# Sparse attention and a two-layer MLP on one core: score pieces of a head pair joined, an order of pieces rewritten, a copy placed later

## The chip, the cores and the metric

One Trainium2 chip, one of its cores. The metric is the device time of one execution in microseconds (us). Twelve runs of the kernel before gave a median of 329.03 us (328.61 to 331.29).

## What is computed

Attention over 8 batches, 8 heads, 576 positions and head size 64. Heads 0 to 3 are *local* (a query sees the 32 positions up to itself), heads 4 to 7 are *strided* (a query sees earlier positions with the same remainder modulo 32). The result, with heads side by side, is a matrix of 4608 rows and 512 columns, which goes through two matrix products with a leaky activation between them.

```python
scores = scale * np.matmul(q, k.transpose(0, 1, 3, 2))
mask_local = (rel >= 0) & (rel < stride)
mask_strided = (rel >= 0) & (pos[None, :] % stride == pos[:, None] % stride)
attn = softmax(where(mask, scores, -1e9))
x = matmul(attn, v).transpose(0, 2, 1, 3).reshape(B * S, H * D)
h = x @ w_in
g = np.maximum(h, 0.0) + alpha * np.minimum(h, 0.0)
out = g @ w_out
```

## The kernel before

**Units.** Heads are taken in pairs; pair g = 4*batch + hp, where hp 0 and 1 are local, 2 and 3 strided. The two heads of a pair lie on partitions 0 to 63 and 64 to 127 of qT and kT. Only blocks that the mask leaves are computed: 6 query blocks of 96 (local) or 8 of 72 (strided) per head. The MLP works in 9 chunks of 512 rows; chunk n needs the attention result up to its last row. `xT`, a ring of four batches, carries the attention result, transposed, from one to the other; its second index is hp.

**A pair's pieces.**
- T, `transpose_piece` and `tails` (L221 to L273): q and k of two pairs are transposed on TensorE into banks of the PSUM pool "ps" (three banks), then copied by DVE and ScalarE. From batch 2 on (`DX`) strided q and k are transposed by DMA instead (`load_d`, `transpose_d`, on SP's queue).
- S, `score_piece` (L275 to L329), two per pair: matmuls with 64 rows, one head on the upper and one on the lower half of the array (L295). Then an exp on ScalarE: one instruction of 576 columns (L319) from the double bank "sp" (pool "pb", one buffer) or, while `wide` is on and for every second piece, two of 288 (L316) from two banks of the pool "ph". In batches 0 and 1 the mask is added by two further matmuls (L311); later GpSimd (POOL) multiplies the exps by a 0/1 mask (L329).
- P, `pv_piece` (L331 to L357), two or three per pair: exps times V with a column of ones (L345) into a "ps" bank; DVE takes the reciprocal of the sum (L352) and multiplies (L354) into x16.
- X: `x_piece` (L359) transposes x16 on TensorE and copies it to xT, by ScalarE for strided (L366) and by DVE for local pairs (L370). For hp 0, 1 and 2 of batches 2 and up a transposing DMA does it: `x_dma` (L372) on SP's queue, straight into xT for local pairs, and for hp 2 into `xs`, which ScalarE copies to xT (`x_copy`, L380, L383).

**MLP pieces.** `lin1_piece` (L534): four matmuls of 512 columns (L544), one for each hp, into one of three banks of "ph"; ScalarE computes relu(-h) (L554), and DVE combines (L557). The DVE half is kept in `late` and issued by the next `attn_step`. `lin2_piece` (L563): four matmuls (L585); every fourth is followed by ScalarE's copy (L590) and the store (L591).

**Order.** The program order of each engine is the order of the Python calls (`keep`). Batch 0 runs alone at the start, with warm matmuls (L607) between its pieces. Batch 1 is woven into chunk 0's lin2 pieces. `alone(u0, u1, ahead)` (L406) writes out the order of these two batches. From batch 2 on the loop of L449 feeds the pieces of each step g in the order S(g,0), P(g-1,0), T q, X(g-2), S(g,1), P(g-1,1), T k, P(g-1,2), and hangs loads, casts, `x_dma`, `transpose_d` and `x_copy` on them. `attn_step` (L524) issues one piece; the loop of L708 issues a batch's pieces evenly over a chunk's 32 MLP pieces, at half density in the lin1 half. During chunk n it issues batch n + 1.

Of the kernel before, what the change touches and what calls it, by code (L numbers as in the profile page):

```python
# [9 lines left out]
F32 = mybir.dt.float32  # L10
F16 = mybir.dt.float16
ALU = mybir.AluOpType
AF = mybir.ActivationFunctionType
# [18 lines left out]
def kernel(  # L32
# [140 lines left out]
    def cast_copy(eng, o, i):  # L173
        if eng == "act":
            keep(nc.scalar.copy(o, i))  # L175
        elif eng == "dve":
            keep(nc.vector.tensor_copy(o, i))  # L177
        else:
            keep(nc.gpsimd.tensor_copy(o, i))  # L179
# [9 lines left out]
    def over_v(b, eng):  # L189

        v16 = vls[b % 2]
        cast_copy(eng, v16[0:32, 1:24, :], v16[96:128, 0:23, :])
# [82 lines left out]
    def score_piece(P, i):  # L275
# [52 lines left out]
            m = (mstr if P.strided else mother).unsqueeze(1).to_broadcast([r, 2 * n // w, w])  # L328
        keep(nc.gpsimd.tensor_tensor(ev, ev, m, op=ALU.mult))  # L329

    def pv_piece(P, a):  # L331
        if P.x16 is None:
            if P.xd and P.strided:
                P.x16 = x16s
            else:
                P.x16 = xpool.tile([128, 1024], F16, tag="x16", name="x16")
        v16 = cast16[(P.b, P.strided, "v")]
        grp = P.pgroups[a]
        r = 72 if P.strided else 128
        pv = pspool.tile([128, 512], F32, tag="ps", name="pv")  # L340
        nb = 2 * len(grp)
        for x in range(nb):
            t, hh = grp[x // 2], x % 2
            et, c = P.et[(t, hh)]
            keep(nc.tensor.matmul(  # L345
                pv[:, 65 * x : 65 * x + 65], et[0:r, c : c + 128],
                v16[0:r, 2 * P.pr + hh, t, :] if P.strided else v16[:, 6 * (2 * P.pr + hh) + t, :],
                start=(x == 0), stop=(x == nb - 1), skip_group_check=True))
        w = P.w
        rc = rpool.tile([128, 8], F32, tag="rc", name="rc")  # L350
        pvv = pv[0:w, 0 : 65 * nb].rearrange("r (c e) -> r c e", e=65)
        keep(nc.vector.reciprocal(rc[0:w, 0:nb], pvv[:, :, 64]))  # L352
        c0 = 128 * grp[0]
        keep(nc.vector.tensor_tensor(  # L354
            P.x16[0:w, c0 : c0 + 64 * nb].rearrange("r (c e) -> r c e", e=64),
            pvv[:, :, 0:64],
            rc[0:w, 0:nb].unsqueeze(2).to_broadcast([w, nb, 64]), op=ALU.mult))  # L357

    def x_piece(P):  # L359
        xp = pspool.tile([128, 1024], F16, tag="ps", name="xp")  # L360
        for t in range(P.n):
            keep(nc.tensor.transpose(  # L362
                xp[:, P.w * t : P.w * t + P.w], P.x16[0 : P.w, 128 * t : 128 * t + 128], ident[0 : P.w, 0 : P.w]))
        base = (P.b % 4) * S
        if P.strided:
            keep(nc.scalar.copy(  # L366
                xT[:, P.hp, base : base + S].rearrange("r (p t) -> r p t", t=8),
                xp[:, 0:576].rearrange("r (t p) -> r p t", t=8)))
        else:
            keep(nc.vector.tensor_copy(xT[:, P.hp, base : base + S], xp[:, 0:576]))  # L370

    def x_dma(P):  # L372
        base = (P.b % 4) * S
# [7 lines left out]
    def x_copy(P):  # L381
        base = (P.b % 4) * S
        keep(nc.scalar.copy(  # L383
            xT[:, P.hp, base : base + S].rearrange("r (p t) -> r p t", t=8),
            P.xs[:, :, 0:72].rearrange("r t p -> r p t")))
# [5 lines left out]
    def feed(fn, g):  # L391
        pieces.append((g, fn))

    def T(u, nm):
        return lambda: transpose_piece(u, nm)

    def Sc(g, i):
        return lambda: score_piece(pairs[g], i)

    def Pv(g, i):  # L400
        return lambda: pv_piece(pairs[g], i)

    def X(g):
        return lambda: x_piece(pairs[g])

    def alone(u0, u1, ahead):  # L406

        A, L = (2 * u0, 2 * u0 + 1), (2 * u1, 2 * u1 + 1)
        feed(T(u0, "q"), -1)
        feed(T(u0, "k"), -1)  # L410
        for g in A:
            for i in range(2):
                feed(Sc(g, i), -1)
        if ahead:
            feed(T(u1, "q"), -1)
            feed(T(u1, "k"), -1)
            for i in range(2):
                feed(Sc(L[0], i), -1)
        for g in A:
            for i in range(3):  # L420
                feed(Pv(g, i), -1)
        if not ahead:
            feed(T(u1, "q"), -1)
            feed(X(A[0]), -1)
            feed(T(u1, "k"), -1)
            feed(X(A[1]), -1)
            for i in range(2):
                feed(Sc(L[0], i), -1)
        for i in range(2):
            feed(Sc(L[1], i), -1)  # L430
        if ahead:
            for g in A:
                feed(X(g), -1)
        for g in L:
            for i in range(2):
                if g == L[0] and i == 0:
                    feed(lambda: (over_v(u0 // 2, "dve"), pv_piece(pairs[L[0]], 0)), -1)
                else:
                    feed(Pv(g, i), -1)
        for g in L:  # L440
            feed(X(g), -1)

    alone(1, 0, True)
    end0 = len(pieces)
    alone(3, 2, True)
    end1 = len(pieces)


    for g in range(7, npair + 2):  # L449
        c = g // 4  # L450
        a, p, t = g, g - 1, g + 1
        okA = 8 <= a < npair
        okP = 8 <= p < npair
        okT = 8 <= t < npair and (t % 4 == 0 or t < 4 * DX and t % 2 == 0)
        nP = len(pairs[p].pgroups) if okP else 0
        seq = []
        if okA:
            seq.append(("S", Sc(a, 0)))
        if okP:
            seq.append(("P", Pv(p, 0)))  # L460
        if okT:
            seq.append(("T", T(t // 2, "q")))
        if 8 <= g - 2 < npair and not pairs[g - 2].xd:
            seq.append(("X", X(g - 2)))
        if okA:
            seq.append(("S2", Sc(a, 1)))
        if okP:
            seq.append(("P", Pv(p, 1)))
        if okT:
            seq.append(("Tk", T(t // 2, "k")))  # L470
        if nP == 3:
            seq.append(("P", Pv(p, 2)))
        if not seq:
            seq.append(("N", lambda: None))

        todo = [(c, pr) for pr in range(2)] if g % 4 == 0 and 8 <= g < npair else []

        if g % 4 == 1 and 9 <= g and c + 1 < B:
            todo = [(c + 1, nm) for nm in "qk"]
        lastP = max([i for i, z in enumerate(seq) if z[0] == "P"], default=len(seq) - 1)  # L480
        copyP = next((i for i, z in enumerate(seq) if z[0] == "S2"), 0)
        nslots = [i for i, z in enumerate(seq) if z[0][0] != "S"] or list(range(len(seq)))
        for i, (kind, fn) in enumerate(seq):
            extra = []
            if todo and i in nslots:
                left = len([z for z in nslots if z >= i])
                cnt = -(-len(todo) // max(1, left))
                extra = [todo.pop(0) for _ in range(min(cnt, len(todo)))]

            def run(fn=fn, extra=extra, g=g, c=c, kind=kind, lastp=(i == lastP), copyp=(i == copyP)):  # L490
                fn()
                for b, pr in extra:
                    if pr in ("q", "k"):
                        cast_l(b, pr)
                        if b + 1 < B:
                            load_qk(b + 1, False, pr)
                        continue
                    cast_v(b, pr, "pool")
                    if pr == 1 and b + 1 < B:
                        load_v(b + 1, True)  # L500
                if kind == "Tk" and g % 4 == 3 and c + 3 < B:
                    load_tail(c + 3, False)
                if lastp:
                    if 4 * DX <= g - 1 < npair and pairs[g - 1].xd:
                        x_dma(pairs[g - 1])
                    if g % 4 == 0 and DX <= c < B:
                        transpose_d()
                    if g % 4 == 2 and DX <= c and c + 1 < B:
                        load_d(c + 1)
                    if g % 4 == 2 and c + 2 < B:  # L510
                        load_v(c + 2, False)
                if copyp and 4 * DX <= g - 2 < npair and pairs[g - 2].xd and pairs[g - 2].strided:
                    x_copy(pairs[g - 2])
            feed(run, g - 2 if kind == "X" else -1)

    pos = {"i": 0}
# [7 lines left out]
    def attn_step(end):  # L524
        if pos["i"] < end:
            pieces[pos["i"]][1]()
            pos["i"] += 1
        while late:
            late.pop(0)()


    gTs = {}
# [222 lines left out]
```

The softmax here doesn't subtract the row's maximum and nothing guards it: scores larger than these inputs give would overflow.

## Time and profile before

| | us |
|---|---|
| median of 12 runs | 329.03 |
| the profiled execution, its own time | 329.14 |
| its span, first to last instruction | 327.20 |
| batch 0 alone, until the first lin1 matmul | 0 to 26.7 |
| chunk 0: lin1, then lin2 with batch 1 | 26.7 to 40.8, 40.8 to 65.2 |
| chunk 1 with batch 2 | 65.2 to 101 |
| one later chunk with a batch, from 136.5 to 169.9 | 33.4 |
| chunks 7 and 8, without attention | 268.1 to the end |

Busy times by engine over the span are 317.4 us for TensorE's matmuls (PE), 182.8 for DVE, 172.5 for ScalarE (ACT) and 141.2 for POOL; the granted TensorE clock is 1.00 throughout. In the lines that follow, a timeline row gives the start, the duration, engine, source line and tiles of one instruction or of a run of like ones (xN), and in brackets how long the engine was idle before and for whom. A group row gives busy time and mean. A row of waits gives engine and tile that waited, whom it waited for, the total in us, how often, and the longest. PEld is TensorE's weight load.

### The profile page before, as it was taken

What the parts mean: (1) busy time and instruction counts of PE and PEld (TensorE: products, weight loads), DVE (VectorE), ACT (ScalarE), POOL (GpSimd) and SP (SyncE); (2) the same over time, 40 slices, a digit from 0 to 9 for tenths busy, and PEclk for the clock granted to TensorE, in tenths of its full rate; (3) what the DMA queues carried; (4) which work ended last, traced back from release to release, by engine and by line L of the source; (5) the groups of instructions that cost most, each with busy time, mean ns of one, the idle gap of its engine ahead of it and who ended that gap; (6) DMA issues with size and microseconds to landing.
All of it is one profiled execution on the core that took longest, in us unless ns stands there. A gap on an engine that the chain in (4) does not pass through costs nothing.

```text
span 327.2 us, 6269 instructions
## 1 busy us (share of the span) xinstructions
PE 317.4 (97%) x2493; PEld 161.7 (49%) x2493; DVE 182.8 (56%) x358; ACT 172.5 (53%) x295; POOL 141.2 (43%) x152
## 2 busy tenths in 40 slices
PE   7899999999998999999999999999999999999995
PEld 2454445554553445444568754445444454444444
DVE  5477835577543882388328833783377338505801
ACT  2744663368446754575467645764567346415610
POOL 8832396307996365736573638342513300000000
PEclk9999999999999999999999999999999999999999
DMA  7999999795498879695968496635440220021011
GB/s 223 193 206 207 248 202 181 110 266 155 94 162 138 220 78 155 98 232 68 165 107 223 53 135 123 114 38 106 119 75 3 52 89 29 1 88 40 2 64 64
DMA packets 77596, 40.32 MB, mean 123 GB/s; under 512 B 58480, under 2 KB 69248, under 8 KB 77568
## 3 DMA queue, kind: packets, MB, share of 16 engines
q0 software_dynamic: 41728, 17.38, 53.9%
q1 hardware_dynamic: 35840, 22.55, 28.9%
q8 instruction: 19, 0.31, 0.5%
q14 instruction: 9, 0.07, 0.1%
HBM read 38.01 MB, written 9.44 MB: 145 GB/s over the span
## 4 chain that ended last, share of the span: by engine, by line
PE 92%; DVE 2%; ACT 2%; DMA 2%; issue 1%; SPq 0%; DVEq 0%; ACTq 0%
PE hps L544 38%; PE ops L585 37%; PE sp L295 4%; PE pv L345 4%; PE tp L235 2%; DMA ql<-in_q_dram 2%; PE wps L607 1%; PE ops L577 1%; PE xp L362 1%; DVE x L354 1%; PE sph L311 1%; PE sp L311 1%; ACT kT L175 1%; DVE qT L177 1%; PE sph L295 1%
## 5 line engine op out<-in xcount | busy, mean ns | idle before, releaser
L585 PE MATMUL ops<-wout,gT 128*128 128x512 f16 x560 | 137.7, 379 | 0.0
L557 DVE SCALAR_TENSOR_TENSOR gT<-neg,oma,hps 128x512 f16<-128x512 f32 x144 | 106.0, 745 | 55.1 <-ACT neg L554 47.6
L544 PE MATMUL hps<-xT,win 128*128 128x512 f16 (+1 forms) x640 | 133.5, 358 | 1.8 <-ACT xT L366 1.2
L554 ACT ACTIVATE neg<-hps 128x512 f32<-128x512 f32 x144 | 86.0, 597 | 41.0 <-PE hps L544 39.5
L329 POOL TENSOR_TENSOR et<-et,consts 128x576 f16<-128x576 f16 (+1 forms) x48 | 61.1, 1275 | 92.3 <-ACT et L319 92.2
L544 PEld LDWEIGHTS <-win 128*128 128x128 f16 x640 | 59.6, 98 | 58.2 <-issue 3.2
L585 PEld LDWEIGHTS <-gT 128*128 128x128 f16 x560 | 48.4, 97 | 45.5
L319 ACT ACTIVATE et<-sp 72x576 f16<-72x576 f32 (+1 forms) x56 | 36.1, 646 | 45.0 <-PE sp L295 36.7
L352 DVE RECIPROCAL rc<-pv 72x6 f32<-72x6 f32 (+2 forms) x80 | 14.8, 185 | 51.2 <-PE pv L345 51.2
L590 ACT COPY osb<-ops 128x512 f32<-128x512 f32 x35 | 20.5, 586 | 31.6 <-PE ops L585 30.9
L354 DVE TENSOR_TENSOR x<-pv,rc 96x384 f16<-96x384 f32 (+2 forms) x62 | 33.0, 532 | 2.1
L345 PEld LDWEIGHTS <-et 72*128 72x128 f16 (+1 forms) x448 | 23.2, 98 | 16.2 <-DVE x L354 1.1
L295 PEld LDWEIGHTS <-kT 64*128 64x128 f16 x448 | 10.8, 95 | 25.8 <-issue 20.7
L295 PE MATMUL sp<-qT,kT 64*128 64x72 f16 (+1 forms) x392 | 17.0, 201 | 1.9 <-ACT kT L175 1.9
L607 PE MATMUL wps<-wrm 128*128 128x512 f16 x44 | 16.4, 448 | 1.2 <-DVE wrm L619 1.2
L345 PE MATMUL pv<-vs,et 72*128 72x65 f16 x256 | 15.3, 194 | 0.1
L167 POOL DMA_DIRECT2D vl<-in_v_dram x8 | 11.2, 1398 | 9.1 <-PE pv L345 8.0
L179 POOL COPY vs<-stv 72x1024 f16<-72x1024 f16 x14 | 14.4, 1034 | 0.0
L177 DVE COPY qT<-tp 128x1024 f16<-128x1024 f16 (+1 forms) x10 | 10.1, 1011 | 7.7 <-PE tp L235 7.7
L383 ACT COPY xT<-xs 128x576 f16<-128x576 f16 x6 | 7.8, 1300 | 8.2 <-DMA xs<-x16s 8.2
L345 PE MATMUL pv<-vl,et 128*128 128x65 f16 x192 | 10.8, 194 | 0.0
L175 ACT COPY kT<-tp 128x1024 f16<-128x1024 f16 (+1 forms) x10 | 8.4, 843 | 3.9 <-PE tp L235 3.9
(72 smaller groups left out, 162.5 us busy)
## 6 DMA issues: line engine op xcount, KB each, us to landing
out_dram<-osb SPq DMA_DIRECT2D x35, 256.0 KB, 2.3
ql<-in_q_dram SPq DMA_DIRECT2D x6, 512.0 KB, 4.7
kl<-in_k_dram SPq DMA_DIRECT2D x6, 512.0 KB, 5.2
stv<-in_v_dram POOLq DMA_DIRECT2D x8, 288.0 KB, 6.3
vl<-in_v_dram POOLq DMA_DIRECT2D x6, 384.0 KB, 10.1
win<-in_moe_w_in_dram POOLq DMA_DIRECT2D x4, 512.0 KB, 10.3
wout<-in_moe_w_out_dram POOLq DMA_DIRECT2D x4, 512.0 KB, 17.5
qsd<-in_q_dram POOLq DMA_DIRECT2D x6, 288.0 KB, 5.9
```

What stands on the lines that cost most here:

```text
L295: keep(nc.tensor.matmul(sps[y][:, w * x : w * x + w], P.kT[hf, k0 : k0 + 128], P.qT[hf, q0 : q0 + w], start=(x == 0), stop=(x == len(grp) ...
L319: keep(nc.scalar.activation(ev.rearrange("r (y c) -> r y c", y=2), sp[0:r, :, 0:n], AF.Exp, scale=SCALE))
L329: keep(nc.gpsimd.tensor_tensor(ev, ev, m, op=ALU.mult))
L345: keep(nc.tensor.matmul(pv[:, 65 * x : 65 * x + 65], et[0:r, c : c + 128], v16[0:r, 2 * P.pr + hh, t, :] if P.strided else v16[:, 6 * (2 * ...
L352: keep(nc.vector.reciprocal(rc[0:w, 0:nb], pvv[:, :, 64]))
L354: keep(nc.vector.tensor_tensor(P.x16[0:w, c0 : c0 + 64 * nb].rearrange("r (c e) -> r c e", e=64), pvv[:, :, 0:64], rc[0:w, 0:nb].unsqueeze ...
L544: keep(nc.tensor.matmul(hps[:, dst : dst + w], win16[:, kk, 128 * m : 128 * m + 128], xT[:, kk, src : src + w], start=(kk == 0 and x == 0) ...
L554: keep(nc.scalar.activation(neg, hps, AF.Relu, scale=-1.0))
L557: keep(nc.vector.scalar_tensor_tensor(gTs[n][:, m, :], neg, oma[:, m : m + 1], hps, op0=ALU.mult, op1=ALU.add))
L585: keep(nc.tensor.matmul(ops, gTs[n][:, kf, 128 * mt : 128 * mt + 128], wout16[:, kf, :], start=(kf == 0), stop=(kf == 15)))
L590: keep(nc.scalar.copy(osb, ops))
L607: keep(nc.tensor.matmul(wps, wrm[:, 0:128], wrm, start=True, stop=True))
```

## The change

Five edits:

1. From batch 2 on a new `score_both` computes both score pieces of a pair one after the other, where S(g,0) stood; S(g,1) is gone from the step. The first half uses the double bank "sp" and one exp of 576 columns, as before. The second half uses two banks of the pool "ps" and two exps of 288, which are put in `defer` and issued one at each following `attn_step` (the first at the end of the same step). `pv_piece` issues any that are outstanding for its own pair first. A pair's attention has one piece less, so the pieces of a batch are spread over the chunk at a lower density.
2. `alone` is rewritten: the PVs of the strided pairs stand between the transposes and scores of the local ones, and the local PVs between the x transposes.
3. In batches 0 and 1 the copy of pair hp 0 to xT goes to ScalarE instead of DVE.
4. `x_copy` is issued after the first piece of step g for pair g - 3; before, it was after S(g,1) for pair g - 2.
5. The local V of a batch is loaded at step 4c + 1 for batch c + 1, where it was step 4c + 2 for batch c + 2; it uses POOL's queue as before.

```diff
+    defer, defer_et = [], {}
+
+    def score_both(P):
+        w, r = P.w, 72 if P.strided else 128
+        for i in range(2):
+            et = ets[ectr["i"] % NE]
+            ectr["i"] += 1
+            if i:
+                sps = [pspool.tile([128, 512], F32, tag="ps", name="sph") for _ in range(2)]
+            else:
+                sp = pbpool.tile([128, 2, 512], F32, tag="sp", name="sp")
+                sps = [sp[:, y] for y in range(2)]
...
+            if i == 0:
+                keep(nc.scalar.activation(
+                    ev.rearrange("r (y c) -> r y c", y=2), sp[0:r, :, 0:n], AF.Exp, scale=SCALE))
+                keep(nc.gpsimd.tensor_tensor(mv, mv, m, op=ALU.mult))
+                continue
+
+            def ex(y):
+                keep(nc.scalar.activation(
+                    ev[:, n * y : n * y + n], sps[y][0:r, 0:n], AF.Exp, scale=SCALE))
+                if y:
+                    keep(nc.gpsimd.tensor_tensor(mv, mv, m, op=ALU.mult))
+
+            defer_et["et"] = et
+            defer.extend([lambda: ex(0), lambda: ex(1)])
+
     def pv_piece(P, a):
+        while defer and any(P.et[z][0] is defer_et["et"] for z in P.et):
+            defer.pop(0)()
...
-            keep(nc.vector.tensor_copy(xT[:, P.hp, base : base + S], xp[:, 0:576]))
+            cast_copy("act" if P.b < NEARLY and P.hp == 0 else "dve",
+                      xT[:, P.hp, base : base + S], xp[:, 0:576])
...
+        fns = [T(u0, "q"), T(u0, "k")] + [Sc(g, i) for g in A for i in range(2)]
+        fns += [Pv(A[0], 0), T(u1, "q"), Pv(A[0], 1), T(u1, "k"), Pv(A[0], 2), Sc(L[0], 0), Sc(L[0], 1)]
+        fns += [lambda: (over_v(u0 // 2, "dve"), pv_piece(pairs[A[1]], 0)), Sc(L[1], 0), Pv(A[1], 1)]
+        fns += [Sc(L[1], 1), Pv(A[1], 2), Pv(L[0], 0), X(A[0]), Pv(L[0], 1), X(A[1])]
+        fns += [Pv(L[1], 0), Pv(L[1], 1), X(L[0]), X(L[1])]
...
-            seq.append(("S", Sc(a, 0)))
+            seq.append(("S", lambda a=a: score_both(pairs[a])))
...
-        if okA:
-            seq.append(("S2", Sc(a, 1)))
...
-                    if g % 4 == 2 and c + 2 < B:
-                        load_v(c + 2, False)
-                if copyp and 4 * DX <= g - 2 < npair and pairs[g - 2].xd and pairs[g - 2].strided:
-                    x_copy(pairs[g - 2])
+                    if g % 4 == 1 and DX < c and c + 1 < B:
+                        load_v(c + 1, False)
+                if first and 4 * DX <= g - 3 < npair and pairs[g - 3].xd and pairs[g - 3].strided:
+                    x_copy(pairs[g - 3])
...
         while late:
             late.pop(0)()
+        if defer:
+            defer.pop(0)()
```

The order of `alone` before (A are the two strided pairs, L the two local ones): T q and T k of A, four scores of A, T q and T k of L, two scores of the first L, six PVs of A, two scores of the second L, X of both A, four PVs of L (with `over_v`, a copy of V's overlap, before the first), X of both L.

More of the change, by code (lines that the diff above doesn't have):

```diff
@@ L329, in score_piece @@
         keep(nc.gpsimd.tensor_tensor(ev, ev, m, op=ALU.mult))
+    defer, defer_et = [], {}
[9 more added lines that the diff above has]
+                sps = [sp[:, y] for y in range(2)]
+            grp = P.sgroups[i]
+            n = w * len(grp)
+            for x, t in enumerate(grp):
+                if P.dx:
+                    q0 = k0 = 80 * (4 * (2 * P.pr + t % 2) + t // 2)
+                else:
+                    q0, k0 = w * t, 32 + 72 * t if P.strided else 96 * t
+                for y in range(2):
+                    hf = slice(64 * y, 64 * y + 64)
+                    keep(nc.tensor.matmul(
+                        sps[y][:, w * x : w * x + w], P.kT[hf, k0 : k0 + 128],
+                        P.qT[hf, q0 : q0 + w], start=(x == 0), stop=(x == len(grp) - 1),
+                        skip_group_check=True))
+                    P.et[(2 * (t // 2) + y, t % 2) if P.strided else (t, y)] = (et, n * y + w * x)
+            ev = et[0:r, 0 : 2 * n]
+            if not P.strided and i == 0:
+                mv = ev.rearrange("r (y c) -> r y c", y=2)
+                m = mfirst.unsqueeze(1).to_broadcast([r, 2, n])
+            else:
+                mv = ev.rearrange("r (c f) -> r c f", f=w)
+                m = (mstr if P.strided else mother).unsqueeze(1).to_broadcast([r, 2 * n // w, w])
+            if i == 0:
[10 more added lines that the diff above has]
+            defer.extend([lambda: ex(0), lambda: ex(1)])
@@ L404, in X, with alone @@
         return lambda: x_piece(pairs[g])
-    def alone(u0, u1, ahead):
+    def alone(u0, u1):
         A, L = (2 * u0, 2 * u0 + 1), (2 * u1, 2 * u1 + 1)
[L409 to L443, printed above, removed]
+        fns = [T(u0, "q"), T(u0, "k")] + [Sc(g, i) for g in A for i in range(2)]
[3 more added lines that the diff above has]
+        fns += [Pv(L[1], 0), Pv(L[1], 1), X(L[0]), X(L[1])]
+        for fn in fns:
+            feed(fn, -1)
+    alone(1, 0)
     end0 = len(pieces)
-    alone(3, 2, True)
+    alone(3, 2)
     end1 = len(pieces)
@@ L480 @@
         lastP = max([i for i, z in enumerate(seq) if z[0] == "P"], default=len(seq) - 1)
-        copyP = next((i for i, z in enumerate(seq) if z[0] == "S2"), 0)
         nslots = [i for i, z in enumerate(seq) if z[0][0] != "S"] or list(range(len(seq)))
@@ L488, with run @@
                 extra = [todo.pop(0) for _ in range(min(cnt, len(todo)))]
-            def run(fn=fn, extra=extra, g=g, c=c, kind=kind, lastp=(i == lastP), copyp=(i == copyP)):
+            def run(fn=fn, extra=extra, g=g, c=c, kind=kind, lastp=(i == lastP), first=(i == 0)):
                 fn()
```

## The prediction, on record before the result

> **What bounds the kernel now.** I read the page first (busy shares and the chain that ended last), then the waits, then TensorE's own order of time.
>
> ```profile
> PE 317.4 (97%) x2493; PEld 161.7 (49%) x2493; DVE 182.8 (56%) x358; ACT 172.5 (53%) x295; POOL 141.2 (43%) x152
> PE 92%; DVE 2%; ACT 2%; DMA 2%; issue 1%; SPq 0%; DVEq 0%; ACTq 0%
> ```
>
> TensorE (PE) is busy 97% of 327.2 us and makes 92% of the chain; no other engine passes 56%. Only two things shorten the kernel: time that PE spends on its own account, and the few places where it waits. The waits show the first kind:
>
> ```profile
> PEld L295 <- issue: 20.7, 54, 0.4
> ```
>
> 54 times the weight load of a score matmul stood still with no semaphore to blame. In TensorE's order of time around two score visits and a PV piece:
>
> ```profile
> 138.31 0.81 PE L544 MATMUL hps<-xT,win 128*128 128x512 f16 x3
> 139.05 0.30 PE L295 MATMUL sp<-qT,kT 64*128 64x96 f16 x6
> 139.29 0.61 PE L544 MATMUL hps<-xT,win 128*128 128x512 f16 x2
> ...
> 141.03 0.35 PE L345 MATMUL pv<-vl,et 128*128 128x65 f16 x6
> 141.21 1.89 PE L544 MATMUL hps<-xT,win 128*128 128x512 f16 x8
> 143.03 0.30 PE L295 MATMUL sp<-qT,kT 64*128 64x72 f16 x8
> 143.27 0.61 PE L544 MATMUL hps<-xT,win 128*128 128x512 f16 x2
> ```
>
> A 512-column matmul starts every 0.216 us. Three from 138.31 free the array at 138.96; the scores start at 139.05: 0.095 us lost. They are three couples of 96 columns, each couple side by side on the two row halves; the last couple starts at 139.15 and streams 0.04, yet L544 starts at 139.29: again 0.095 lost. The second visit loses as much, the PV piece nothing (141.03 + 8 x 0.216 and its 0.18 lead to 142.94, and the scores start at 143.03). So a visit to the row-tiled mode costs 0.19 us beside its matmuls.
>
> The second kind is one place of some size:
>
> ```profile
> 101.12 0.59 PE L544 MATMUL hps<-xT,win 128*128 128x512 f16 x2
> 102.10 0.38 PE L544 MATMUL hps<-xT,win 128*128 128x512 f16 x1 [0.39 <-ACT xT L383]
> 103.67 1.02 PE L544 MATMUL hps<-xT,win 128*128 128x512 f16 x4 [1.19 <-ACT xT L366]
> ```
>
> Chunk 2's third matmul is due at 101.55 and starts at 102.10, its fourth is due at 102.32 and starts at 103.67: 0.55 + 1.35 = 1.9 us lost. ScalarE is behind it:
>
> ```profile
> 100.75 1.30 ACT L383 COPY xT<-xs 128x576 f16<-128x576 f16 x1 [4.23 <-DMA xs<-x16s]
> 101.96 0.58 ACT L590 COPY osb<-ops 128x512 f32<-128x512 f32 x1
> 102.44 0.65 ACT L319 ACTIVATE et<-sp 128x576 f16<-128x576 f32 x1
> 102.98 0.64 ACT L366 COPY xT<-xp 128x576 f16<-128x576 f16 x1
> ```
>
> x_copy (L383) stood 4.23 us for its transposing DMA with an output copy, an exp and the copy of pair 11 queued behind it. The DMA was issued at 93.98 and took 6.7 us here, against a median of 3.2.
>
> **The Trainium skill.** "TensorEngine Tiling (Array Packing)", Key Properties: changing the tiling mode, not just the tile, drains TensorE. The trace agrees and prices it: 0.095 us on each side. "ScalarE: Activation LUTs", What ACT_TABLE_LOAD costs: an ACTIVATE with immediate scale and bias takes 186 ns + 0.833 ns per element, and back-to-back ones overlap by 93 ns. The trace has 650 ns for 576 columns and 400 to 410 for 288, with starts 0.1 us earlier than the ends: agrees. "TensorE: Matmul & The Clock Gate", its table: ScalarE's queue is a strict FIFO; agrees with the four rows above. "DMA: Bandwidth & Descriptors", Issuing engines are not separate DMA queues: all transfers share 16 engines; the 6.7 us landing beside a V load issued at 89.19 fits that, without proving it.
>
> **The change part by part.**
>
> *One score visit for a head pair, 24 pairs of batches 2 to 7.* 48 visits become 24; none of the 48 touches another in PE's order. 24 x 0.19 = 4.5 us, all on PE, no cover: a clear gain. Matmuls stay the same in number and size. Bounds: 4.5, and 0 if the drain were paid between the two halves. I take 4.5. It adds ScalarE work: 24 exps of 576 columns become 48 of 288, 24 x (2 x 0.405 - 0.645) = 4.0 us on an engine that is 53% busy. Queued behind them is the relu L554, which frees one of three hps banks through L557. After a visit: relu of the piece before, exp 0.54 apart, half exp 0.31, then the next relu, due 1.13 us after the visit's end (0.864 of matmul + 0.27) and free at about 0.93. The second half exp is held back one piece and fits before the following relu. So no wait, with 0.2 us to spare. If ScalarE's starts were a full duration apart, about 0.25 us would be lost in each visit of the lin1 halves, 11 visits: 2.8 us (first rival).
>
> *PSUM.* The second half now takes two of the three ps banks, which PV, transposes and x results share. Along the order after the change each bank's reader has at least one 0.864 us lin piece plus other PE work before reuse; a PV's readers take 0.19 + 0.55 us, the half exps are done about 1.5 us after the visit. I cost it at nothing; the cover is the lin piece. The exception is chunk 1, where the k transposes of batch 3 now stand one lin2 piece (not two) ahead of the first visit that reads them: about 1.25 us on PE, against 1.75 from the start of such transposes to the scores at 72.58/74.33. Loss 0.5 us.
>
> *x_copy one pair later.* In chunk 1 it moves from the third piece after its DMA's issue to the fifth; five lin2 pieces (4.3), a visit (0.5), PVs (0.5) and the exp ahead make about 6.3 us, and the V load of 89.19 is no longer issued there. The 1.9 us go; I leave 0.1 for the half exps that it now delays, as the bank they free is needed by pair 11's x transposes. If the landing stays at 6.7 from the issue, up to 1.2 comes back. Also in chunk 1 the first visit comes one lin1 piece later, so two waits of scores (0.24 at 74.34, 0.09 at 77.70) vanish. With the 0.5 from above: 1.9 + 0.3 - 0.5 - 0.1 = 1.6 us gain (bounds 0.4 to 2.2).
> In the last batch nothing follows pair 31, so x_copy of pair 30 is now issued *after* pair 31's copy:
>
> ```profile
> 267.01 0.42 PE L362 MATMUL xp<-consts,x 72*128 72x72 f16 x8
> 267.27 1.03 PE L585 MATMUL ops<-wout,gT 128*128 128x512 f16 x4
> 268.13 0.81 PE L544 MATMUL hps<-xT,win 128*128 128x512 f16 x3
> ```
>
> L366 starts at 267.47; x_copy 0.52 later, 1.30 long, done at 269.3. Chunk 7's third matmul (kk = 2) wants it at 268.13 + 0.43 = 268.56. New wait: 0.8 us (0.5 to 1.3).
>
> *Batch 0.* Before, PE waits for kT 0.97 us at 16.15 with nothing else to do, and later DVE cannot keep up with ten PVs nearly in a row (0.69 us each on DVE, 0.40 on PE with the warm matmul): 0.25, 0.14, 0.28, 0.21, 0.55 and 0.27 us. Sum 2.7. After, PVs fill the first hole and DVE works from 14 us. Walking the new order with these durations, I lose about 0.5 where the tail transposes wait for the q bank (DVE copy, then ScalarE copy, now behind a PV's DVE work), 0.3 at the first chunk's second matmul and 0.3 at the last x transposes; lin1 starts near 25.3 instead of 26.68. One DVE copy (0.45) going to ScalarE is in that. I take 1.2 (0 to 1.9): the pv needs V's cast at 13.4, only 0.2 before it is due, and V's local load must land by 18 instead of 22.
>
> *Batch 1.* Two waits, 0.44 at 45.10 and 0.54 at 51.59. The first stays, the second shrinks: 0.4 gain (-0.3 to 0.8).
>
> *V load moved* to three steps later: on POOL's queue and the DMA engines; V is needed a whole batch (33 us) later and lands within 11.3. Nothing.
>
> **Sum.** 4.5 + 1.6 + 1.2 + 0.4 - 0.8 = 6.9 us. The profiled execution took 329.14 (span 327.20 and 1.94 around it), so 320.3 span and 322.2; the median of the runs, 329.03, is 0.1 less: 322.1.
>
> **Rivals.** (1) ScalarE backlog, 2.8 us as above: 324.9. Against it: starts overlap in the trace, and L544 waited only 1.8 us in all. (2) The drain belongs to each change of PSUM banks or half, so that a merged visit keeps it: 322.1 + 4.5 = 326.6. Against: couples within a visit follow each other at 0.03 to 0.05 us although they alternate banks. (3) The ps pool turns the gain over: with two of three banks held until the deferred half exps have run, each visit or the PV behind it waits for one exp of 0.405 us: 24 x 0.405 = 9.7, 331.8. It decides from 6.9/24 = 0.29 us per visit. Against: in the steady chunks the new order never reuses a bank less than 1.2 us of PE work after it was filled, and ScalarE is half idle. (4) Start and chunk 1 give nothing (inputs or the xs transfer still late): 322.1 + 1.2 + 1.6 = 324.9.
>
> **How the numbers follow.** Main case 0.66; (1) 0.11; (2) 0.08; (3) 0.05; (4) 0.08; no change 0.02. Low end: all upper bounds, 0.7 + 0.6 + 0.4 + 0.3 more, gives 320.1; the range up to 325.4 takes in (1) and (4) with half a microsecond and leaves out (2), (3) and no change, 0.15. A measurement of this kernel can tell about 0.2% (0.7 us) from no change: faster 0.93, within 0.02, slower 0.05.
>
> **What would show it.** Right: 24 fewer score visits and the issue wait of L295 down by about 24 x 0.4; a steady chunk at 32.6 instead of 33.4 us; no PE wait for L383's successor at chunk 2, but one of 0.8 at chunk 7; lin1's first matmul near 25.3. Wrong: PE waits on ACT exps or on pv's readers inside visits (3), hps waits in lin1 stretches (1), or chunks still at 33.4 (2).

## The result, and the profile after

| | before | after |
|---|---|---|
| median, us | 329.07 (32 runs) | 323.58 (8 runs, 323.33 to 323.74) |
| ratio, with 95% interval | | 0.983 [0.981, 0.984] |
| profiled execution: its time, its span | 329.14, 327.20 | 323.41, 321.63 |
| first lin1 matmul starts at | 26.68 | 25.17 |
| chunk 0 / 1 / 2 | 38.55 / 35.89 / 35.25 | 38.39 / 35.69 / 32.90 |
| chunk 3 / 4 / 5 / 6 | 33.35 / 33.52 / 33.35 / 31.54 | 32.91 / 33.04 / 32.90 / 30.78 |
| chunk 7 | 27.63 | 28.42 |

5.5 us were gained where 6.9 were forecast. (A chunk lasts from its first lin1 matmul to that of the next; the stretch from chunk 8 on is 31.43 us in both.)

The page after, in the rows that the forecast began with (busy us, share of the span, instructions; then the engines' shares of the chain that ended last):

```profile
PE 313.3 (97%) x2493; PEld 162.4 (50%) x2493; DVE 183.5 (57%) x356; ACT 172.8 (54%) x321; POOL 140.6 (44%) x152
PE 87%; issue 5%; POOL 2%; DVE 2%; DMA 2%; ACT 1%; SPq 0%; POOLq 0%; ACTq 0%; DVEq 0%
```

TensorE still bounds the kernel: the same 2493 matmuls, 97% busy. ScalarE has 26 more instructions and 0.3 us more busy time. Its exps, added one by one, take 46.8 us instead of 42.6, close to the 4.0 more of the forecast; the busy time hardly grows because ScalarE's instructions overlap more (their durations sum to 185.1 us after and 179.6 before). TensorE's weight loads, in the waits after:

```profile
PEld L353 <- issue: 8.9, 22, 0.4
PEld L569 <- issue: 3.9, 10, 0.9
PEld L295 <- issue: 3.0, 10, 0.4
```

Before, 54 loads of score weights stood still for "issue", 20.7 us in all; now it is 22 + 10, 11.9 us: 8.8 less, where the forecast's sign was about 24 x 0.4 = 9.6. The second row belongs to lin1 and is the part that the forecast missed. A visit and the stretch ahead of it, in TensorE's order of time (chunk 3):

```profile
138.18 1.90 PE L569 MATMUL hps<-xT,win 128*128 128x512 f16 x8
139.91 0.35 PE L396 MATMUL pv<-vl,et 128*128 128x65 f16 x6
140.10 2.95 PE L569 MATMUL hps<-xT,win 128*128 128x512 f16 x12
142.89 0.35 PE L396 MATMUL pv<-vl,et 128*128 128x65 f16 x6
143.07 2.75 PE L569 MATMUL hps<-xT,win 128*128 128x512 f16 x12
145.76 0.30 PE L353 MATMUL sp<-qT,kT 64*128 64x72 f16 x8
145.90 0.30 PE L353 MATMUL sph<-qT,kT 64*128 64x72 f16 x8
```

The two halves of a visit follow each other without a hole (145.76 and 145.90). From the 512-column matmul ahead of a visit (its start plus 0.216 us) to the start of the next one after the visit, the median was 0.329 us (local) or 0.332 (strided) for each of two visits before, and is 0.457 or 0.462 for the joined one: 0.20 us less per pair, 24 x 0.20 = 4.8 us. But the twelve lin1 matmuls from 140.10 show 2.95 us where those from 143.07 show 2.75: the first twelve lost 0.20. That is the new wait, two per chunk in chunks 2 to 6; in chunk 6 the kernel before had two as well, so eight of the ten are new.

The stall at the start of chunk 2 is gone:

```profile
99.25 2.75 PE L569 MATMUL hps<-xT,win 128*128 128x512 f16 x12
```

Before, the third and fourth matmuls of that chunk came 0.55 and 1.35 us late. What is left as waits of TensorE's matmuls in the middle and at the end (engine and tile, whom it waited for, us, times, longest):

```profile
PE hps L569 <- ACT xT L435: 0.6, 1, 0.6
PE pv L396 <- POOL et L375: 0.4, 1, 0.4
...
PE xp L413 <- ACT et L372: 0.2, 1, 0.2
```

The first is the end of the last batch, as forecast:

```profile
261.12 0.64 ACT L417 COPY xT<-xp 128x576 f16<-128x576 f16 x1 [2.39 <-PE xp L413]
...
261.65 1.31 ACT L435 COPY xT<-xs 128x576 f16<-128x576 f16 x1
261.78 0.59 PE L569 MATMUL hps<-xT,win 128*128 128x512 f16 x2
...
263.01 2.32 PE L569 MATMUL hps<-xT,win 128*128 128x512 f16 x10 [0.63 <-ACT xT L435]
```

The third matmul of chunk 7 (kk = 2) was due at 262.21 and starts at 263.01, when x_copy of pair 30, behind the copy of pair 31, is done: 0.80 us.

**Where the new 0.20 us comes from.** One such place in chunk 2, all engines that touch lin1:

```profile
101.84 0.35 PE L396 MATMUL pv<-vl,et 128*128 128x65 f16 x6
...
102.02 2.95 PE L569 MATMUL hps<-xT,win 128*128 128x512 f16 x12
102.04 0.60 ACT L579 ACTIVATE neg<-hps 128x512 f32<-128x512 f32 x1 [0.27 <-PE hps L569]
102.47 0.18 DVE L403 RECIPROCAL rc<-pv 96x6 f32<-96x6 f32 x1
102.69 0.55 DVE L405 TENSOR_TENSOR x<-pv,rc 96x384 f16<-96x384 f32 x1
103.08 0.60 ACT L579 ACTIVATE neg<-hps 128x512 f32<-128x512 f32 x1 [0.45 <-PE hps L569]
103.16 2.16 DVE L582 SCALAR_TENSOR_TENSOR gT<-neg,oma,hps 128x512 f16<-128x512 f32 x3
...
103.95 0.53 PEld L569 LDWEIGHTS <-win 128*128 128x128 f16 x3 [0.32 <-issue]
```

The lin1 piece ahead of the PV has its relu (L579) from 102.04 to 102.64. Its second half, DVE's combine (L582), is kept in `late` and issued by the next `attn_step` *after* that step's piece, here a PV; so it stands in DVE's queue behind the PV's reciprocal and multiplication and starts at 103.16, not at 102.64. It ends at about 103.9. Only then is its hps bank free, of which there are three; the third lin1 piece after the PV (102.02 + 2 x 0.864 = 103.75) wants the same bank and starts at 103.95. ScalarE is not late: each of its relus waited for TensorE (the brackets). The Trainium skill's "TensorE: Matmul & The Clock Gate", Part 1, lists ScalarE's and VectorE's queues as strict FIFOs; the order on DVE above agrees.

So three theories went to the chip: (A) the order on DVE, and not ScalarE, costs the 0.2 us; (B) the joined visits' gain is the drain between modes, and not a lower cost of something else; (C) what removed the 1.9 us at chunk 2, the later copy (edit 4) or, as a rival, the V load that no longer runs beside the xs transfer (edit 5). The kernel before, measured beside each group of experiments, had medians of 329.06 to 329.22 us; the intervals are those of the ratio to it. When a number is called a chunk's, it is of the profiled execution.

### The profile page after: what moved, and what is told of

Same layout as the page of the kernel before. It is cut to its first block, busy times and chain, and to the rows that moved or that the text cites. A ratio compares the mean times of both kernels' runs of the same rounds, so it can differ in the third digit from the quotient of the medians.

```text
span 321.6 us, 6320 instructions
## 1 busy us (share of the span) xinstructions
PE 313.3 (97%) x2493; PEld 162.4 (50%) x2493; DVE 183.5 (57%) x356; ACT 172.8 (54%) x321; POOL 140.6 (44%) x152
## 4 chain that ended last, share of the span: by engine, by line
PE 87%; issue 5%; POOL 2%; DVE 2%; DMA 2%; ACT 1%; SPq 0%; POOLq 0%; ACTq 0%; DVEq 0%
PE ops L610 36%; PE hps L569 35%; PE pv L396 4%; PE tp L235 2%; PE wps L632 2%; PE sp L353 2%; DMA ql<-in_q_dram 2%; PE ops L602 1%; PE xp L413 1%; PE sp L311 1%; PE sph L311 1%; PE sph L353 1%; DVE x L405 1%; PE sp L295 1%; POOL vs L179 1%
## 5 line engine op out<-in xcount | busy, mean ns | idle before, releaser
L582 DVE SCALAR_TENSOR_TENSOR gT<-neg,oma,hps 128x512 f16<-128x512 f32 x144 | 106.3, 745 | 52.6 <-ACT neg L579 44.5
L610 PE MATMUL ops<-wout,gT 128*128 128x512 f16 x560 | 135.3, 379 | 0.0
L569 PE MATMUL hps<-xT,win 128*128 128x512 f16 (+1 forms) x640 | 132.7, 358 | 1.1 <-ACT xT L435 0.6
L579 ACT ACTIVATE neg<-hps 128x512 f32<-128x512 f32 x144 | 86.0, 597 | 38.8 <-PE hps L569 38.8
L569 PEld LDWEIGHTS <-win 128*128 128x128 f16 x640 | 60.2, 98 | 60.2 <-issue 3.9
L610 PEld LDWEIGHTS <-gT 128*128 128x128 f16 x560 | 49.2, 97 | 47.2
L396 PEld LDWEIGHTS <-et 72*128 72x128 f16 (+1 forms) x448 | 24.1, 98 | 16.6 <-POOL et L375 0.9
L366 ACT ACTIVATE et<-sp 128x576 f16<-128x576 f32 (+1 forms) x24 | 15.5, 645 | 11.3 <-PE sp L353 11.3
L372 ACT ACTIVATE et<-sph 128x288 f16<-128x288 f32 (+1 forms) x48 | 18.6, 408 | 0.0
L353 PEld LDWEIGHTS <-kT 64*128 64x128 f16 x336 | 7.1, 95 | 9.9 <-issue 8.9
L417 ACT COPY xT<-xp 128x576 f16<-128x576 f16 x10 | 6.4, 639 | 6.5 <-PE xp L413 6.5
```

The costliest lines, as they stand in the source:

```text
L372: keep(nc.scalar.activation(ev[:, n * y : n * y + n], sps[y][0:r, 0:n], AF.Exp, scale=SCALE))
L396: keep(nc.tensor.matmul(pv[:, 65 * x : 65 * x + 65], et[0:r, c : c + 128], v16[0:r, 2 * P.pr + hh, t, :] if P.strided else v16[:, 6 * (2 * ...
L569: keep(nc.tensor.matmul(hps[:, dst : dst + w], win16[:, kk, 128 * m : 128 * m + 128], xT[:, kk, src : src + w], start=(kk == 0 and x == 0) ...
L579: keep(nc.scalar.activation(neg, hps, AF.Relu, scale=-1.0))
L582: keep(nc.vector.scalar_tensor_tensor(gTs[n][:, m, :], neg, oma[:, m : m + 1], hps, op0=ALU.mult, op1=ALU.add))
L610: keep(nc.tensor.matmul(ops, gTs[n][:, kf, 128 * mt : 128 * mt + 128], wout16[:, kf, :], start=(kf == 0), stop=(kf == 15)))
```

## The experiments

**1. The combine ahead of the PV.** In the changed kernel:

```diff
     def attn_step(end):
+        while late:
+            late.pop(0)()
         if pos["i"] < end:
             pieces[pos["i"]][1]()
             pos["i"] += 1
-        while late:
-            late.pop(0)()
         if defer:
             defer.pop(0)()
```

> The changed kernel with one edit: in each attention step the kept-back DVE combine of the MLP piece before is issued ahead of the step's attention piece, not after it. Theory DVE order (the new 0.2 us waits of lin1 matmuls come because a PV's reciprocal and multiply, 0.7 us, stand ahead of the combine that frees the hps bank, and three lin1 pieces follow): all ten waits of about 0.2 us in chunks 2 to 6 go, 1.6 to 2.0 us, so about 321.7 us. Theory ScalarE backlog (the added half exps hold back the relu): the waits stay, 323.6 us.

Measured: 322.06 us (321.50 to 322.93, 6 runs), 0.978 [0.975, 0.980] of before. Chunks 2 to 5 are 32.5 to 32.7 us instead of 32.9 to 33.0, and of the ten 0.2 us waits one is left, in chunk 6. At the same place:

```profile
100.79 2.47 DVE L582 SCALAR_TENSOR_TENSOR gT<-neg,oma,hps 128x512 f16<-128x512 f32 x3 [3.03 <-ACT neg L579]
...
101.68 0.35 PE L396 MATMUL pv<-vl,et 128*128 128x65 f16 x6
...
101.86 2.75 PE L569 MATMUL hps<-xT,win 128*128 128x512 f16 x12
...
103.18 0.18 DVE L403 RECIPROCAL rc<-pv 96x6 f32<-96x6 f32 x1
```

The three combines now run before the reciprocal, and the twelve matmuls take 2.75 us. ScalarE's work is unchanged, so A holds: DVE's order cost 1.5 us, by the medians and by the 0.39 us that each of chunks 2 to 5 is shorter.

**2. The old density of pieces.** A piece that does nothing stands where S(g,1) stood, so that a batch again has as many pieces as before.

```diff
+        if okA:
+            seq.append(("S2", lambda: None))
```

> The changed kernel with an empty piece where the second score piece stood, so that a batch's pieces are spread as densely as before and at most two lin1 pieces follow each other. Theory DVE order with runs of three lin1 pieces: the hps waits of chunks 2 to 5 go although the order on DVE and the half exps stay, 1.6 us, about 322.0 us (chunk 1 may move by half a microsecond either way). Theory ScalarE backlog: the same half exps stand ahead of the same relus, so the waits stay and the time is 323.6 us or more.

Measured: 325.87 us (325.06 to 326.99, 6 runs), 0.989 [0.987, 0.992]. A miss. One of the two hps waits in each of chunks 2 to 5 went, as expected of a denser order (fewer places where three lin1 pieces follow a PV). But x transposes now wait in five places, and chunk 5 has another, long wait:

```profile
PE sp L353 <- DMA kT<-ksd: 1.8, 1, 1.8
...
PE xp L413 <- ACT et L372: 0.8, 5, 0.2
```

The x transposes (L413) need the ps bank that the last half exps (L372) free, and in front of these stands the 1.3 us x_copy. In the changed kernel the same copy and half exps end before the transposes are due (only chunk 1 waits). The 1.8 us for a transposing DMA appear in no other profile here. SyncE took 5.01 us to issue that transfer; in this kernel three of the six k transfers took 4.5 to 5.0 us to issue, in the changed kernel 1.9 to 3.4. The runs don't show why. The density has a cost in one place and a use in another; it isn't the simple loss that was expected.

**3 and 4. The drain between the halves.** In the changed kernel, one small matmul into the second half's bank before its first score matmul: with 128 rows (TensorE leaves the row-tiled mode and returns) or, as a control, with 64 (it doesn't leave). The scores overwrite its values.

```diff
             if i:
+                keep(nc.tensor.matmul(
+                    sps[0][:, 0:64], ident[0:128, :], ident[0:128, 0:64],
+                    start=True, stop=True, skip_group_check=True))
```

The control has `ident[0:64, ...]` in both places.

> The changed kernel with one extra matmul of 128 rows and 64 columns between the two halves of each joined score visit (its result is overwritten by the scores). Theory drain by mode: each of 24 visits is split into two, 0.19 us of drains and 0.03 us of matmul each, 5.3 us in all: 328.9 us. Theory that the joined visit still pays between its halves: only the matmul, 0.7 us: 324.3 us.

> The same extra matmul with 64 rows, so that TensorE stays in the row-tiled mode. Both theories: 24 x 0.03 = 0.7 us of matmul, 324.3 us. It is the control for the kernel with 128 rows: the difference of the two is the price of 24 changes of mode and back, 4.6 us by the theory of a drain by mode, nothing by the other.

Measured: 328.76 us (328.28 to 329.27, 20 runs), 0.998 [0.997, 0.999], against 324.23 us (324.06 to 324.64, 4 runs), 0.984 [0.981, 0.987]. TensorE's order of time around one visit, 128 rows first, then 64:

```profile
129.34 0.30 PE L357 MATMUL sp<-qT,kT 64*128 64x96 f16 x6
129.57 0.20 PE L347 MATMUL sph<-consts 128*128 128x64 f16 x1
129.71 0.30 PE L357 MATMUL sph<-qT,kT 64*128 64x96 f16 x6
129.94 1.90 PE L614 MATMUL ops<-wout,gT 128*128 128x512 f16 x8
```

```profile
128.06 0.30 PE L357 MATMUL sp<-qT,kT 64*128 64x96 f16 x6
128.19 0.19 PE L347 MATMUL sph<-consts 64*128 64x64 f16 x1
128.20 0.31 PE L357 MATMUL sph<-qT,kT 64*128 64x96 f16 x6
128.44 1.90 PE L614 MATMUL ops<-wout,gT 128*128 128x512 f16 x8
```

From the first score to the next MLP matmul it is 0.60 us against 0.38, and each of chunks 2 to 5, with four visits, is 0.86 us longer: 0.22 a visit. Over the whole run the small matmul with 128 rows costs 4.5 us more in 24 places, 0.19 each; the average is lower because chunk 1, with six visits, is only 0.64 us longer: a PV and the x transposes, which wait there anyway, wait less. The columns themselves don't explain it: the control's visits are 0.026 us longer than the changed kernel's, about what 64 columns take at the pace of the MLP matmuls (64/512 x 0.216 = 0.027, an estimate). What is left is the change of mode. This is what the Trainium skill's "TensorEngine Tiling (Array Packing)", Key Properties, says without a price: a change of the mode drains the array. B holds, and the second rival of the prediction falls.

**5. The order of batches 0 and 1 alone.** The kernel before with edits 2 and 3.

```diff
-    def alone(u0, u1, ahead):
+    def alone(u0, u1):
...
+        fns += [Pv(A[0], 0), T(u1, "q"), Pv(A[0], 1), T(u1, "k"), Pv(A[0], 2), Sc(L[0], 0), Sc(L[0], 1)]
...
+            cast_copy("act" if P.b < NEARLY and P.hp == 0 else "dve",
+                      xT[:, P.hp, base : base + S], xp[:, 0:576])
```

> The kernel before with the new order of batches 0 and 1 alone, and the copy of pair hp 0 on ScalarE (edits 2 and 3). If the changed kernel's gain up to chunk 1 (1.5 us ahead of the first lin1 matmul, 0.2 in chunk 0) belongs to these edits: 327.4 us. If it needs the others, or if a later transfer takes it back: 328.5 to 329.1 us.

Measured: 327.49 us (327.25 to 327.65, 7 runs), 0.994 [0.991, 0.996]. lin1 starts at 25.27 instead of 26.68, chunk 0 is 38.38 instead of 38.55, every later chunk as before within 0.12. 1.6 us, as the two terms of the forecast together.

**6. The later x_copy alone.** The kernel before with edit 4.

```diff
-                if copyp and 4 * DX <= g - 2 < npair and pairs[g - 2].xd and pairs[g - 2].strided:
-                    x_copy(pairs[g - 2])
+                if first and 4 * DX <= g - 3 < npair and pairs[g - 3].xd and pairs[g - 3].strided:
+                    x_copy(pairs[g - 3])
```

> The kernel before with x_copy one pair later alone (edit 4). Theory: the 1.9 us at the start of chunk 2 go, 0.8 us at the start of chunk 7 come: 328.0 us. Theory that the gain at chunk 2 comes from the V load that no longer collides with the xs transfer: 1.9 us stay in good part, 329.0 us or more.

Measured: 328.85 us (328.18 to 330.59, 22 runs), 0.997 [0.996, 0.999]. A miss: 0.76 us of chunk 2's stall went, not 1.9, and chunk 7 lost its 0.79. The copy in ScalarE's order of time:

```profile
101.12 1.31 ACT L383 COPY xT<-xs 128x576 f16<-128x576 f16 x1 [2.12 <-DMA xs<-x16s]
```

Before, the copy started at 100.75 and had stood 4.23 us. Issued later, it stands 2.12 us and still starts at 101.12: the transfer, issued at 94.09, landed 7.0 us later. What had been queued behind the copy now runs first, but the copy itself, which chunk 2 needs, is not earlier. So edit 4 isn't what removed the stall, and alone it is worth little: 0.2 to 0.4 us by the medians, nothing by its two chunks, which sum to 0.03 us more.

**7. Edit 5 undone in the changed kernel.**

```diff
-                    if g % 4 == 1 and DX < c and c + 1 < B:
-                        load_v(c + 1, False)
+                    if g % 4 == 2 and c + 2 < B:
+                        load_v(c + 2, False)
```

> The changed kernel with the local V loaded at its old place (edit 5 undone). Theory that the V load slows the xs transfer of chunk 1: it lands 6 to 7 us after its issue again, x_copy waits about 1 us, the x transposes behind it too: 324.3 us. Theory that the load's place is indifferent: xs lands within 5.5 us, 323.6 us.

Measured: 327.74 us (326.24 to 329.08, 14 runs), 0.993 [0.991, 0.995]: 4.2 us slower than the changed kernel, more than either figure expected. Chunk 1 is 38.80 us instead of 35.69; the other chunks are the same within 0.02. (The profiled execution is only 3.1 us of span above the changed kernel's; the runs of this kernel spread over 2.8 us.)

```profile
PE xp L413 <- ACT et L372: 3.3, 1, 3.3
```

ScalarE's order of time there:

```profile
99.64 1.30 ACT L435 COPY xT<-xs 128x576 f16<-128x576 f16 x1 [3.08 <-DMA xs<-x16s]
100.85 0.70 ACT L372 ACTIVATE et<-sph 128x288 f16<-128x288 f32 x2
```

The V load is issued at 88.35, xs at 90.88, and xs lands 8.7 us later. The copy waits for it, the two half exps wait behind the copy, they hold the ps bank, and TensorE stands 3.5 us before the x transposes. With edit 1 the wait for xs is worse than it was before, since a PSUM bank hangs on it.

**8. Edit 5 alone** (the kernel before with the diff of 7 the other way round), **and 9. edits 4 and 5.**

> The kernel before with edit 5 alone (V loaded at step 4c + 1 for batch c + 1), nothing else. Theory A: the V load, in progress while the xs transfer of pair 10 waits for its packets, set the 6.7 us landing; without it xs lands about 3 us after its issue at 94, x_copy starts near 97 instead of 100.75, and the 1.9 us that TensorE lost at the start of chunk 2 go without any change to the place of x_copy: 329.05 - 1.9 = 327.1. Rival B: the other traffic of that stretch (q, k, tails, stores) sets the landing and V only takes its turn: xs still lands later than 6 us after its issue, and the time stays at 329.0 within 0.3.

> The kernel before with edits 4 and 5. Theory A: edit 5 has already removed the stall at chunk 2, so edit 4 adds only its cost at the end, 0.8 us where chunk 7's kk = 2 matmul waits for pair 30's x_copy: 327.1 + 0.8 = 327.9. Rival B: as edit 4 alone, 328.8, with 0.8 and 0.3 us of the stall at the start of chunk 2 left.

Measured: 327.14 us (326.93 to 327.48, 6 runs), 0.994 [0.992, 0.996], and 327.85 us (327.50 to 327.89, 9 runs), 0.996 [0.995, 0.997]. With edit 5 alone chunk 2 falls from 35.25 to 33.35 us and nothing else moves. The copy in ScalarE's order of time, with edit 5 alone:

```profile
97.18 1.31 ACT L383 COPY xT<-xs 128x576 f16<-128x576 f16 x1 [0.62 <-DMA xs<-x16s]
```

The xs transfer lands at most 3.2 us after its issue (6.7 before), and the copy starts 3.6 us earlier than before, from the same place in the order. C is settled for the rival: edit 5 removed the 1.9 us. Edit 4 then only adds its 0.7 us. That all transfers share 16 DMA engines whoever issues them ("DMA: Bandwidth & Descriptors", Issuing engines are not separate DMA queues) is the likely way; the trace has the landing with and without the V load, not the order of packets on an engine.

**10. Edit 4 undone in the changed kernel**, the copy after the second PV piece of step g.

```diff
+        copyP = ([i for i, z in enumerate(seq) if z[0] == "P"] + [0, 0])[1]
...
-                if first and 4 * DX <= g - 3 < npair and pairs[g - 3].xd and pairs[g - 3].strided:
-                    x_copy(pairs[g - 3])
+                if copyp and 4 * DX <= g - 2 < npair and pairs[g - 2].xd and pairs[g - 2].strided:
+                    x_copy(pairs[g - 2])
```

> The changed kernel with edit 4 undone: the copy of xs for pair g - 2 stands after the second PV piece of step g. Theory A: with the V load moved (edit 5) the transfer lands in 2.7 us, in chunk 1 in 5.6, before or at most 1 us after the copy's turn, and what ScalarE then does late is covered; so edit 4 brought nothing in this kernel and cost the 0.8 us at chunk 7: 323.6 - 0.8 = 322.8. Rival B: the 1.3 us copy, standing earlier, holds up exps in each of the six chunks by 0.2 us or more, or chunk 1's stall comes back with 1 us: 323.6 or slower.

Measured: 323.77 us (323.41 to 323.97, 5 runs), 0.983 [0.981, 0.985]. Chunk 7 is back at 27.62 (0.80 us less), but chunk 1 is 1.04 us longer; the five chunks between are equal. The time can't be told from that of the changed kernel. ScalarE's order of time, chunk 1:

```profile
96.26 1.31 ACT L435 COPY xT<-xs 128x576 f16<-128x576 f16 x1 [3.78 <-DMA xs<-x16s]
...
98.50 0.71 ACT L372 ACTIVATE et<-sph 128x288 f16<-128x288 f32 x2
```

In this chunk the transfer lands 5.6 us after its issue even without the V load, and the copy, standing 3.78 us, holds up an exp and the half exps. Of the two sides of this expectation, the one with chunk 1's stall was right.

**11. Both repairs.** The order of experiment 1 (its edit, not shown again), and for pair 30 only the copy after its neighbour's last PV, ahead of pair 31's x transposes.

```diff
-                if first and 4 * DX <= g - 3 < npair and pairs[g - 3].xd and pairs[g - 3].strided:
+                if first and 4 * DX <= g - 3 < npair - 4 and pairs[g - 3].xd and pairs[g - 3].strided:
                     x_copy(pairs[g - 3])
+                if lastp and g == npair:
+                    x_copy(pairs[g - 2])
```

> The changed kernel with the DVE combine ahead of the attention piece, and in the last batch alone x_copy after the last PV, ahead of the x transposes of pair 31. The wait of 0.8 us at chunk 7 goes: 321.3 us, against 322.1 with the combine alone. If x_copy there holds back pair 31's copy by its 1.3 us, a wait of up to 0.5 us takes its place: 321.8 us.

Measured: 321.17 us (321.01 to 321.31, 4 runs), 0.975 [0.971, 0.978]: the fastest here, ahead of both kernels. Chunk 7 is 27.63 us again and chunks 2 to 5 are 32.5 to 32.7.

## Why the prediction was right in the main and 1.4 us short

The forecast's terms against the profiled executions (negative is a gain; the joined visits from the medians above, the hps term from experiment 1, the other terms from the table of chunks with these two taken out):

| term | forecast | measured |
|---|---|---|
| 24 joined visits | -4.5 | -4.8 |
| "no wait" behind the visits (hps) | 0 | +1.5 |
| batch 0, to the first lin1 | -1.2 | -1.5 |
| batch 1, chunk 0 | -0.4 | -0.2 |
| chunks 1 and 2 (hps apart) | -1.6 | -1.3 |
| end, pair 30's copy | +0.8 | +0.8 |
| sum | -6.9 | -5.5 |

*Joined visits.* Right in mechanism and nearly in size. A pair saves 0.20 us where one visit of 0.19 was forecast; experiments 3 and 4 put a change of mode and back at 0.22 us at the visit and 0.19 averaged over the run. What parts 0.20 from 0.22 is open.

*The step that failed* is "So no wait, with 0.2 us to spare". It followed the relu on ScalarE to the visit's exps and stopped at the relu. The bank is freed by the combine on DVE, "through L557" as the text itself says, and DVE's queue holds the PV's 0.7 us ahead of it. The gap to look for was the third lin1 piece after a PV, not the second after a visit. In the order before, such a place came up at two points of chunk 6 (0.20 us each); the order after has ten of them, and the lower density has a part in it (with the old one, in experiment 2, four of the ten went). So a steady chunk is 32.9 us and not 32.6, and 32.5 with the order of experiment 1. "hps waits in lin1 stretches", the prediction's sign for its first rival, did appear. That rival named the right bank, with 2.8 us against 1.5, but the wrong engine: the relus were never late, and experiment 1 took 1.5 us back without touching ScalarE.

*Chunks 1 and 2* came out near the sum with two wrong reasons in it, so the agreement of that term is luck. The 1.9 us were credited to the later copy, and the V load was costed at "Nothing". Experiments 6 and 8 reverse this: edit 5 is worth 1.9 us, edit 4 on its own 0.4 at most. Edit 4 became useful only beside edit 1: undone in the changed kernel, it costs 1.04 us in chunk 1 and gains 0.8 in chunk 7 (experiment 10). The forecast had seen both clues, the V load issued at 89.19 and the 6.7 us landing, and it even said that the load "is no longer issued there"; it costed the edit only by who waits for V, not by who shares the DMA engines with it. Undoing edit 5 in the changed kernel costs 4.2 us (experiment 7). "Nothing" would have needed that no transfer with a waiting engine behind it ran at the same time.
The smaller terms of chunk 1: the two waits of scores for kT, 0.33 together, did vanish. The 0.5 us for k transposes of batch 3 was 0.11 (the visit at 91.03). Not foreseen were 0.54 us in which a PV waits for a mask:

```profile
75.91 2.01 POOL L179 COPY vs<-stv 72x1024 f16<-72x1024 f16 x2
...
77.87 0.81 POOL L159 DMA_DIRECT2D stv<-in_v_dram  x1
...
78.69 1.29 POOL L375 TENSOR_TENSOR et<-et,consts 128x576 f16<-128x576 f16 x1
...
80.04 0.36 PE L396 MATMUL pv<-vl,et 128*128 128x65 f16 x6 [0.38 <-POOL et L375]
```

The half exp ended at 77.83, but POOL's queue had two copies of V and a DMA issue ahead of the mask. And the 0.1 us for half exps behind x_copy was 0.40, at the x transposes of 98.13.

*Batches 0 and 1.* Both signs right; the sizes, 1.2 and 0.4, were 1.5 and 0.2, and alone (experiment 5) they give the 1.6 us of the sum.

*The end.* Right: 0.8 forecast, 0.80 in the trace, and experiment 11 removes it by placing the copy earlier.

*Rivals.* That the drain stays (326.6) is excluded by the visits themselves, 0.20 us shorter per pair, and by experiments 3 and 4. The ps pool that turns the gain over (331.8) is not seen in the steady chunks: no wait on a half exp there. In chunk 1 it is real, 0.40 us, and up to 3.5 when the xs transfer is late. That start and chunk 1 give nothing is excluded by experiments 5 and 8.

Open: why the k transfer of experiment 2 came 1.8 us late, in what way the V load delays the xs transfer, and the 0.02 us between the two prices of a visit.

## What to carry to other kernels

A PSUM bank is free when its last reader has run, so follow each bank to that reader and read everything that is queued ahead of it on its engine; here a step that was on time on ScalarE was late by 0.2 us on DVE, in ten places. A transfer with slack of its own is not free to place: ask which short transfer with a waiting engine behind it runs in the same microseconds, and test the move alone, since a bundle of edits gave the right sum for a wrong reason. Visits to another tiling mode are worth joining when TensorE is the bound, at about 0.2 us each here.

## What the runs showed of the hardware

- A small matmul that changes the tiling mode costs about 0.2 us more than one of the same columns that doesn't (experiments 3 and 4: 0.22 us at the visit, 4.53 us in 24 places over the run).
- The transposing DMA into xs lands 2.7 us after its issue in the median with edit 5 alone, and took 6.7 to 8.7 us in the one batch where a V load of 384 KB was issued 2.5 to 5 us ahead of it (before, experiments 6 and 7). In that same batch without the load beside it, it took 3.1 (experiment 8) and 5.6 us (the changed kernel).
- A lin1 matmul that waits for its bank shows in the waits as its weight load standing 0.3 us for "issue", with no engine named, in chunks 2, 3, 5 and 6. In chunk 4 the same two waits name their engine:

```profile
PEld L569 <- DVE gT L582: 0.6, 2, 0.3
```

It is the combine, as experiment 1 has it. "issue" is thus not always a drain: at L353 it is, at L569 it was a wait.
